# Luna attention and a squared-ReLU layer: batches 0 and 1 loaded together, both attentions first, their hidden tiles in turns

## The chip, the cores and the metric

The kernel runs on one core of a Trainium2 chip. The metric is the device time of one execution in microseconds (us): seven timed runs of the kernel before have a median of 272.58 us (271.35 to 272.79). One further execution was recorded by the hardware profiler; every time of a single instruction in this document comes from such a recorded execution.

The engines of a core work in parallel, each on its own list of instructions, in order. TensorE (PE) multiplies matrices into PSUM, a small memory. ScalarE (ACT) and VectorE (DVE) read PSUM and write SBUF, the large on-chip memory. GpSimd (POOL) here issues the loads, and SyncE (SP) the stores and the transposing transfers. An engine waits for another through semaphores.

## The reference

```python
def sm_attn(qq, kk, vv):
    s = scale * np.matmul(qq, kk.transpose(0, 1, 3, 2))
    s = s - np.max(s, axis=-1, keepdims=True)
    a = np.exp(s)
    a = a / (np.sum(a, axis=-1, keepdims=True) + 1e-09)
    return np.matmul(a, vv)
p_packed = sm_attn(p, k, v)              # 32 packed rows per head
out = sm_attn(q, p_packed, p_packed)     # 576 rows attend to the 32

x = out.transpose(0, 2, 1, 3).reshape(B * S, H * D)
h = x @ w_in
r = np.maximum(h, 0.0)
g = s * (r * r) + b
y = g @ w_out
```

There are 8 batches, 8 heads, 576 rows and 64 columns per head; p has 32 rows per head. x is 4608 x 512, w_in 512 x 2048, w_out 2048 x 512. Inputs and the output are float32, and the loads turn them into bfloat16.

## The kernel before, in words

One batch goes through these helpers; each name stands in the code below.

- `load` (line 93) brings k, q and v of a batch into the SBUF tiles kn, qn and vn, one transfer of 576 KB (as bfloat16) each, on POOL's queue. `load_w_in(ch)` brings a quarter of w_in in two transfers of 256 KB, and `load_w_out(m, m + 4)` a quarter of w_out in one of 512 KB.
- `prep_k` and `prep_q` transpose kn and qn on TensorE, for batches 0 to 2; ACT and DVE copy the result to kT and qT. From batch 3 on, transfers on SP do it (`dma_k`, `dma_q`), from kn and from qr, which is a reordered copy of qn made on DVE (`order_q`; `order_v` does the same for v).
- `first_scores(b, qd)` makes the scores of p against k for half of the heads, and ACT takes the exponential (tile e1). `packed` multiplies by v and DVE writes ppc, with the reciprocal sums rd and rs. `second_scores` makes the scores of q against ppc, and ACT takes the exponential (tile e2). `weights(b, qd)` sums e2 on TensorE, ACT takes Ln (tile ld) and Exp (tile rcd), and DVE multiplies into aT.
- `packed_w1(b, ch)` multiplies ppc by one quarter of w_in, 8 matmuls; the two halves of the result are scaled into pw by ACT and then DVE (both on DVE with `on_act=False`). `packed_w` does two quarters at once.
- `mlp_in(b, m)`, also called through `m1`, makes one of the 16 hidden tiles of a batch: 4 matmuls of 288 columns from pw and aT, ReLU on ACT (tile rlu), the square on DVE (tile gT). The hidden tile m uses quarter m // 4 of pw.
- An `Out` makes 128 rows of y: 16 matmuls of 512 columns over gT and w_out, in steps of any number; then DVE scales and adds (tile ysb) and SP stores. `outs(b)` gives 4 of them for an even batch and 5 for an odd one, and `fill(n)` issues the next n matmuls of those that are waiting.
- `bias_part` sums the rows of w_out, 16 matmuls in all; `idle(n)` issues n matmuls on zeros.

The order on every engine is written by hand: instructions run in program order. Results in PSUM live in `big()` tiles of a pool with three buffers (psh), those of an `Out` in a pool with two (psy). A `big()` tile must be read by ACT or DVE before the third next one can be written.

Lines 128 to 175 give the order of the loads: batch 0, all of w_in, all of w_out, batch 1, then the rest of p. kn, qn, vn, vr and qr have one buffer each, so that a load of the next batch waits for the last reader of the tile before. Eight semaphores are shared by POOL's transfers in turn, so that a transfer also waits for the one eight places ahead of it to land.

Lines 517 to 624 are the beginning, written out step by step: the attention of batch 0, its 16 hidden tiles with the first two Outs and the bias sums between them, then the attention of batch 1 with the remaining two Outs between its steps, its hidden tiles, and the attention of batch 2 between those. From line 626 a loop runs over batches 2 to 7: 16 hidden tiles each, after each hidden tile the steps of the next batch's attention that are set for it, and then `fill(per)`, with per the number of waiting Outs.

Of the kernel before, what the change touches and what calls it, by code (L numbers as in the profile page):

```python
# [14 lines left out]
def kernel(  # L15
# [41 lines left out]

    constp = ctx.enter_context(tc.tile_pool(name="constp", bufs=1))
    wpool = ctx.enter_context(tc.tile_pool(name="wpool", bufs=1))
    rawp = ctx.enter_context(tc.tile_pool(name="rawp", bufs=1))  # L60
    attp = ctx.enter_context(tc.tile_pool(name="attp", bufs=1))
    atp = ctx.enter_context(tc.tile_pool(name="atp", bufs=2))
    smp = ctx.enter_context(tc.tile_pool(name="smp", bufs=2))
# [22 lines left out]
    def big(dt=F32):  # L86
        w = NB if dt == F32 else 2 * NB
        return psh.tile([P, 2, w], dt, tag="h", name="hps")


    kn, qn, vn = {}, {}, {}

    def load(store, src, b, tag, h0=0, h1=H):
        if h0 == 0:
            store[b] = rawp.tile([R, H, NC * D], BF16, tag=tag, name=tag)
        pool.dma_start(
            out=store[b][:, h0:h1, :],
            in_=src[b, h0:h1].rearrange("h (r c) d -> r h (c d)", c=NC),
        )
# [17 lines left out]
    def load_w_out(m0, m1):  # L117
        pool.dma_start(
            out=w_out_sb[:, m0:m1, :],
            in_=moe_w_out[m0 * P:m1 * P, :].rearrange("(m p) d -> p m d", p=P),  # L120
        )
# [17 lines left out]
    bvec = constp.tile([P, 1], F32, name="bvec")  # L139
    sp.dma_start(out=bvec[:], in_=moe_b[0:1].unsqueeze(0).to_broadcast([P, 1]))  # L140
    nc.scalar.preload_act_table_set("natural_log_exp_and_others")
    for ch in range(NCH):
        load_w_in(ch)
    for m in range(0, NFF, 4):
        load_w_out(m, m + 4)

    KW = H * HS + 32
    kT = [constp.tile([P, KW], BF16, name=f"kT{i}") for i in range(2)]
# [17 lines left out]
    def idle(n):  # L166

        t = big()
        for x in range(n):
            mm(t[:, 0, :], zeros[:, 0:P], zeros[:], start=True, stop=True)  # L170

    load(kn, k, 1, "kn")
    load(qn, q, 1, "qn")
    load(vn, v, 1, "vn")
    load_p(2, B)


# [43 lines left out]
        )  # L221

    def order_v(b):
        vr[b] = attp.tile([R, NC, HP, 2, D], BF16, tag="vr", name="vr")
        by_chunk(vr[b], vn[b])

    def order_q(b):
        qr[b] = attp.tile([R, NC, HP, 2, D], BF16, tag="qr", name="qr")
        by_chunk(qr[b], qn[b])

    def prep_q(b, half):
# [53 lines left out]
    def packed(b, qd):  # L285
        i = b % 2
        if qd == 0:
            pps[b] = big()
        pp = pps[b]
        for hp in range(2 * qd, 2 * qd + 2):  # L290
            for c in range(NC):
                if b < N_PE_T:
                    for h2 in range(2):
                        o = hp * 2 * NP + h2 * NP
                        mm(
                            pp[D * h2:D * h2 + D, 0, o:o + NP],
                            vn[b][:, hp + HP * h2, c * D:(c + 1) * D],
                            e1[b][:, h2, c, hp, :],
                            start=(c == 0),
                            stop=(c == NC - 1),  # L300
                            tile_position=(0, D * h2),
                        )
                else:
                    mm(
                        pp[:, 0, hp * 2 * NP:(hp + 1) * 2 * NP],
                        vr[b][:, c, hp, :, :],
                        e1[b][:, :, c, hp, :],
                        start=(c == 0),
                        stop=(c == NC - 1),
                    )  # L310
        for c in range(NC):
            mm(
                pp[:, 1, qd:qd + 1],
                e1[b][:, qd, c, :, :],
                ones1[0:R, :],
                start=(c == 0),
                stop=(c == NC - 1),
            )
        if qd == NQ - 1:
            for h2 in range(2):  # L320
                vec.tensor_copy(
                    out=ppc[i][D * h2:D * h2 + D, :, :],
                    in_=pp[D * h2:D * h2 + D, 0, 0:HP * 2 * NP].rearrange("p (a j) -> p a j", a=HP)[
                        :, :, NP * h2:NP * h2 + NP
                    ],
                )
            rd[b] = smp.tile([P, NQ], F32, tag="rd", name="rd")
            vec.reciprocal(out=rd[b][:], in_=pp[:, 1, 0:NQ])
            rs[b] = smp.tile([P, NQ], F32, tag="rs", name="rs")
            vec.tensor_scalar_mul(out=rs[b][:], in0=rd[b][:], scalar1=scale)  # L330
# [63 lines left out]
    def packed_w1(b, ch, on_act=True):  # L394

        i = b % 2
        if ch == 0:
            pw[b] = ppw.tile([P, NQ, DFF], BF16, tag="pw", name="pw")
        t = big()
        packed_mm(i, ch, [t[:, qd, :] for qd in range(NQ)])  # L400
        dst = pw[b][:, :, ch * NB:(ch + 1) * NB]
        if on_act:
            act.activation(out=dst[:, 0], in_=t[:, 0, :], func=AF.Copy, scale=rd[b][:, 0:1])
        else:
            vec.tensor_scalar_mul(out=dst[:, 0], in0=t[:, 0, :], scalar1=rd[b][:, 0:1])
        vec.tensor_scalar_mul(out=dst[:, 1], in0=t[:, 1, :], scalar1=rd[b][:, 1:2])
# [33 lines left out]
    def bias_part(cps, m):  # L440
        mm(cps, onesb[:], w_out_sb[:, m, :], start=(m == 0), stop=(m == NFF - 1))
        if m == NFF - 1:
            vec.tensor_scalar_mul(out=biasrep[:], in0=cps, scalar1=bvec[:])
# [69 lines left out]
    def m1(b, *ms):  # L513
        for m in ms:
            mlp_in(b, m)
# [16 lines left out]
    packed(0, 1)  # L532
    idle(5)
    second_scores(0)
    packed_w1(0, 0, on_act=False)
    idle(3)
    weights(0, 0)
    weights(0, 1)
    packed_w1(0, 1, on_act=False)
    idle(6)  # L540
    m1(0, 0, 1, 2, 3)
    packed_w1(0, 2, on_act=False)
    m1(0, 4, 5, 6)

    todo = outs(0)
    first, second = todo[0], todo[1]
    bps = big()
    m = 7
    for m0 in range(0, NFF, 4):
        for x in range(m0, m0 + 4):  # L550
            bias_part(bps[:, 0, :], x)
        if m < NFF:
            m1(0, m)
        first.step(4)
        if m < NFF:
            m1(0, m + 1)
        second.step(4)
        if m < NFF:
            m1(0, m + 2)
        if m0 == 0:  # L560
            packed_w1(0, 3, on_act=False)
        m += 3
    loads(2)
    todo = todo[2:]

    def fill(n):
        run_outs(todo, n)

    prep_k(1, 0)
    prep_k(1, 1)  # L570
    fill(4)
    first_scores(1, 0)
    fill(4)
    first_scores(1, 1)
    fill(4)
    prep_q(1, 0)
    prep_q(1, 1)
    fill(4)
    packed(1, 0)
    packed(1, 1)  # L580
    twice_p(2, B)
    fill(5)
    packed_w1(1, 0)
    second_scores(1)
    fill(3)
    packed_w1(1, 1)
    weights(1, 0)
    fill(2)
    weights(1, 1)
    prep_p(2)  # L590
    fill(2)
    packed_w1(1, 2)
    prep_k(2, 0)
    m1(1, 0, 1)
    packed_w1(1, 3)
    m1(1, 2)
    prep_k(2, 1)
    m1(1, 3, 4)
    first_scores(2, 0)
    m1(1, 5, 6)  # L600
    fill(4)
    first_scores(2, 1)
    m1(1, 7, 8)
    prep_q(2, 0)
    prep_q(2, 1)
    m1(1, 9, 10)
    packed(2, 0)
    m1(1, 11)
    packed(2, 1)
    loads(3)  # L610
    m1(1, 12, 13, 14)
    second_scores(2)
    m1(1, 15)
    todo = outs(1)
    packed_w1(2, 0)
    fill(6)
    weights(2, 0)
    fill(4)
    packed_w1(2, 1)
    weights(2, 1)  # L620
    fill(6)
    packed_w1(2, 2)
    fill(4)
    dma_k(3)

    for b in range(2, B):
        a = b + 1
        c = a + 1
        steps = {}

        def at(m, *fs):
            steps.setdefault(m, []).extend(fs)

        d = 3 if b == 2 else 0
        if b == 2:
            at(1, lambda: (packed_w1(2, 3), order_q(3), dma_q(3)))
            at(2, lambda: (prep_p(3), order_v(3)))
        if a < B:
            at(0 + d, lambda: first_scores(a, 0))
            at(1 + d, lambda: first_scores(a, 1))  # L640
            at(3 + d, lambda: packed(a, 0))
            at(4 + d, lambda: packed(a, 1))
            at(6 + d, lambda: second_scores(a))
            at(8 + d, lambda: packed_w(a, 0))
            at(9 + d, lambda: weights(a, 0))
            at(10 + d, lambda: weights(a, 1))
            at(12 + d, lambda: packed_w(a, 1))
        if c < B:
            at(1 + d, lambda: loads(c))
            at(8 + d, lambda: dma_k(c))  # L650
            at(10 + d, lambda: (order_q(c), dma_q(c)))
            at(12 + d, lambda: order_v(c))
            at(14, lambda: prep_p(c))
        if b > 2:
            todo = outs(b - 1)
        per = len(todo)
        for m in range(NFF):
            mlp_in(b, m)
            for f in steps.get(m, []):
                f()  # L660
            fill(per)
        fill(NFF * (NT + 1))
# [31 lines left out]
```

The softmax here doesn't subtract the row's maximum and nothing guards it: scores larger than these inputs give would overflow.

## Time and profile before

| what | us |
|---|---|
| median of 7 runs | 272.58 (271.35 to 272.79) |
| the profiled execution's own time | 270.08 |
| its span, from the first to the last instruction | 268.3 |
| TensorE busy with matmuls in the span | 247.2 (92%) |
| DVE busy | 146.3 (55%) |
| ACT busy | 142.8 (53%) |
| POOL busy | 29.3 (11%) |
| matmuls of the Outs (yps), 544 recorded | 137.2 |
| matmuls of the hidden tiles, 512 recorded | 82.7 |
| matmuls on zeros, 41 recorded | 14.1 |

The span is the time from the first to the last recorded instruction; the execution's own time is 1.8 us longer. Matmuls overlap each other and their ends are modelled, so a group's busy time adds up to more than the time it takes. Where a row of a timeline ends with square brackets, they give how long the engine had been idle before it and what ended the wait. A chain of waits follows the work that ended last back through whatever released each step.

### The profile page before, as it was taken

What the parts mean: (1) busy time and instruction counts of PE and PEld (TensorE: products, weight loads), DVE (VectorE), ACT (ScalarE), POOL (GpSimd) and SP (SyncE); (2) the same over time, 40 slices, a digit from 0 to 9 for tenths busy, and PEclk for the clock granted to TensorE, in tenths of its full rate; (3) what the DMA queues carried; (4) which work ended last, traced back from release to release, by engine and by line L of the source; (5) the groups of instructions that cost most, each with busy time, mean ns of one, the idle gap of its engine ahead of it and who ended that gap; (6) DMA issues with size and microseconds to landing.
All of it is one profiled execution on the core that took longest, in us unless ns stands there. A gap on an engine that the chain in (4) does not pass through costs nothing.

```text
span 268.3 us, 5619 instructions
## 1 busy us (share of the span) xinstructions
PE 247.2 (92%) x2312; PEld 139.5 (52%) x2348; DVE 146.3 (55%) x304; ACT 142.8 (53%) x217; POOL 29.3 (11%) x44
## 2 busy tenths in 40 slices
PE   7787899986989699899999999999999999999993
PEld 2453555644654365465556555665566555555441
DVE  2235854458657745764793559455954574444221
ACT  1045743456977447775855476548753774443000
POOL 8345100211110020030030002000000000000000
PEclk9799999999999999999999999999999999999999
DMA  3999999894792999999979769993731113111332
GB/s 40 197 206 205 205 204 143 148 157 84 129 150 37 184 170 199 128 159 233 168 99 183 194 127 151 125 232 75 132 96 42 39 39 83 39 39 42 78 78 78
DMA packets 54634, 34.32 MB, mean 128 GB/s; under 512 B 27472, under 2 KB 50000, under 8 KB 54608
## 3 DMA queue, kind: packets, MB, share of 16 engines
q0 software_dynamic: 25200, 18.61, 48.1%
q1 hardware_dynamic: 29408, 15.34, 27.4%
q8 instruction: 18, 0.29, 0.4%
q14 instruction: 8, 0.07, 0.1%
HBM read 37.23 MB, written 9.44 MB: 174 GB/s over the span
## 4 chain that ended last, share of the span: by engine, by line
PE 78%; ACT 8%; DVE 5%; DMA 5%; issue 3%; POOL 0%; DVEq 0%; ACTq 0%; POOLq 0%
PE yps L71 42%; PE hps L71 34%; ACT rlu L82 3%; DMA pn<-in_p_dram 3%; PE hps L74 2%; DMA kT<-kn 2%; ACT rcd L82 2%; ACT ld L82 1%; DVE pw L82 1%; ACT e L82 1%; DVE ysb L82 1%; ACT pw L82 1%; DVE qr L82 1%; DVE gT L82 1%; DVE aT L82 1%
## 5 line engine op out<-in xcount | busy, mean ns | idle before, releaser
L71 PE MATMUL yps<-w_out_sb,gT 128*128 128x512 bf16 x544 | 137.2, 379 | 2.8 <-issue 1.6
L82 ACT ACTIVATE rlu<-hps 128x576 bf16<-128x576 f32 x128 | 82.4, 649 | 73.0 <-PE hps L71 65.6
L82 DVE TENSOR_TENSOR gT<-rlu 128x576 bf16<-128x576 bf16 x128 | 58.0, 456 | 70.3 <-ACT rlu L82 69.3
L71 PE MATMUL hps<-aT,pw 128*128 128x288 bf16 x512 | 82.7, 286 | 4.4 <-DVE pbd L82 1.7
L71 PEld LDWEIGHTS <-gT 128*128 128x128 bf16 x576 | 52.8, 98 | 50.2 <-issue 5.8
L71 PEld LDWEIGHTS <-pw 128*128 128x128 bf16 x512 | 49.2, 98 | 39.0 <-issue 4.9
L82 DVE SCALAR_TENSOR_TENSOR ysb<-yps,svec,biasrep 128x512 f32<-128x512 f32 x36 | 26.8, 747 | 14.3 <-PE yps L71 14.0
L82 DVE TENSOR_SCALAR pw<-hps,rd 128x512 bf16<-128x512 f32 (+1 forms) x26 | 24.4, 950 | 3.1 <-ACT pw L82 2.0
L82 ACT ACTIVATE e<-hps 96x768 bf16<-96x768 f32 x16 | 12.8, 802 | 19.4 <-PE hps L71 19.3
L82 ACT ACTIVATE pw<-hps,rd 128x1024 bf16<-128x1024 f32 (+1 forms) x18 | 16.6, 923 | 4.0 <-PE hps L71 3.9
L82 POOL DMA_DIRECT2D kn<-in_k_dram x9 | 6.9, 769 | 104.5 <-DMA kT<-kn 55.2
L82 DVE TENSOR_TENSOR aT<-e,rcd 128x576 bf16<-128x576 bf16 x16 | 12.1, 758 | 10.6 <-ACT rcd L82 10.5
L71 PE MATMUL hps<-zeros 128*128 128x512 bf16 x41 | 14.1, 480 | 2.2 <-DVE zeros L82 1.3
L82 ACT ACTIVATE e<-hps,rs 128x576 bf16<-128x576 f32 x16 | 10.9, 738 | 3.7 <-PE hps L71 3.7
L71 PE MATMUL hps<-w_in_sb,ppc 64*32 64x512 bf16 x256 | 11.6, 383 | 0.9 <-ACT e L82 0.4
L71 PE MATMUL hps<-pbd,kT 128*128 128x64 bf16 x192 | 8.6, 194 | 2.9 <-DMA kT<-kn 2.0
L82 ACT ACTIVATE rcd<-ld 128x576 f32<-128x576 f32 x16 | 10.9, 682 | 0.5
L82 ACT ACTIVATE ld<-hps 128x576 f32<-128x576 f32 x16 | 10.3, 643 | 0.9 <-PE hps L71 0.9
L71 PEld LDWEIGHTS <-kT 128*128 128x128 bf16 x192 | 7.9, 99 | 5.2 <-DMA kT<-kn 2.3
L71 PEld LDWEIGHTS <-ppc 64*32 64x32 bf16 x384 | 4.1, 89 | 9.0 <-issue 7.4
L71 PEld LDWEIGHTS <-zeros 128*128 128x128 bf16 x44 | 4.6, 113 | 7.9 <-issue 4.7
L82 POOL DMA_DIRECT2D qn<-in_q_dram x8 | 6.2, 776 | 12.7 <-PE hps L74 9.6
(45 smaller groups left out, 115.5 us busy)
## 6 DMA issues: line engine op xcount, KB each, us to landing
qn<-in_q_dram POOLq DMA_DIRECT2D x8, 576.0 KB, 10.8
vn<-in_v_dram POOLq DMA_DIRECT2D x8, 576.0 KB, 12.5
out_dram<-ysb SPq DMA_DIRECT2D x24, 192.0 KB, 2.3
kn<-in_k_dram POOLq DMA_DIRECT2D x7, 576.0 KB, 7.3
out_dram<-ysb SPq DMA_DIRECT2D x24, 128.0 KB, 2.5
w_in_sb<-in_moe_w_in_dram POOLq DMA_DIRECT2D x8, 256.0 KB, 12.9
w_out_sb<-in_moe_w_out_dram POOLq DMA_DIRECT2D x4, 512.0 KB, 13.1
out_dram<-ysb SPq DMA_DIRECT2D x24, 64.0 KB, 2.0
```

What stands on the lines that cost most here:

```text
L71: return tc.keep_in_program_order(nc.tensor.matmul(*a, **kw))
L74: return tc.keep_in_program_order(nc.tensor.transpose(*a, **kw))
L82: return lambda *a, **kw: tc.keep_in_program_order(f(*a, **kw))
```

## The change

Three things change in the beginning; the loop over batches 2 to 7 is as it was, but for one call.

First the loads. Batch 1 comes directly after batch 0: kn and qn, then the first quarter of w_in, vn, the first quarter of w_out, and then quarters of w_in and w_out in turns. kn, qn, vn, vr and qr no longer have a buffer each; they draw from one pool of five buffers of the same size.

Then the order of the beginning. After the second scores of batch 0 the attention of batch 1 starts, and the two attentions are interleaved. Of the hidden tiles of batch 0 only four are made before the weights of batch 1; the other twelve alternate with those of batch 1, with two matmuls of an Out (`step(2)`) after ten of the hidden tiles of batch 0. The bias sums come after all the hidden tiles, and the attention of batch 2 after that, between the rest of the first two Outs, the other two Outs of batch 0 and ten matmuls of the Outs of batch 1. `packed_w1` in this part uses ACT for its first half. There are 42 matmuls on zeros where there were 44.

Last, for batches 0 to 2 `packed` writes both halves of the heads to the same columns of PSUM, and one copy of 128 partitions writes ppc instead of two of 64.

```diff
-    rawp = ctx.enter_context(tc.tile_pool(name="rawp", bufs=1))
+    rawp = ctx.enter_context(tc.tile_pool(name="rawp", bufs=5))
...
+    def raw(name):
+        return rawp.tile([R, S // R * DM], BF16, tag="raw", name=name)[:]
+
     def load(store, src, b, tag, h0=0, h1=H):
         if h0 == 0:
-            store[b] = rawp.tile([R, H, NC * D], BF16, tag=tag, name=tag)
+            store[b] = raw(tag).rearrange("r (h x) -> r h x", h=H)
...
-    for ch in range(NCH):
+    load(kn, k, 1, "kn")
+    load(qn, q, 1, "qn")
+    load_w_in(0)
+    load(vn, v, 1, "vn")
+    load_w_out(0, 4)
+    for ch in range(1, NCH):
         load_w_in(ch)
-    for m in range(0, NFF, 4):
-        load_w_out(m, m + 4)
+        load_w_out(4 * ch, 4 * ch + 4)
...
-    load(kn, k, 1, "kn")
-    load(qn, q, 1, "qn")
-    load(vn, v, 1, "vn")
     load_p(2, B)
...
-        vr[b] = attp.tile([R, NC, HP, 2, D], BF16, tag="vr", name="vr")
+        vr[b] = raw("vr").rearrange("r (c h x d) -> r c h x d", c=NC, h=HP, x=2)
...
-        qr[b] = attp.tile([R, NC, HP, 2, D], BF16, tag="qr", name="qr")
+        qr[b] = raw("qr").rearrange("r (c h x d) -> r c h x d", c=NC, h=HP, x=2)
...
-                        o = hp * 2 * NP + h2 * NP
                         mm(
-                            pp[D * h2:D * h2 + D, 0, o:o + NP],
+                            pp[D * h2:D * h2 + D, 0, hp * NP:(hp + 1) * NP],
...
+            if b < N_PE_T:
+                vec.tensor_copy(out=ppc[i][:].rearrange("p a j -> p (a j)"), in_=pp[:, 0, 0:HP * NP])
+            else:
...
     second_scores(0)
-    packed_w1(0, 0, on_act=False)
+    prep_k(1, 0)
+    prep_k(1, 1)
+    weights(0, 0)
+    first_scores(1, 0)
+    weights(0, 1)
+    first_scores(1, 1)
+    loads(2)
     idle(3)
-    weights(0, 0)
-    weights(0, 1)
-    packed_w1(0, 1, on_act=False)
-    idle(6)
-    m1(0, 0, 1, 2, 3)
-    packed_w1(0, 2, on_act=False)
-    m1(0, 4, 5, 6)
-
+    packed_w1(0, 0)
+    prep_q(1, 0)
+    prep_q(1, 1)
+    m1(0, 0, 1)
+    idle(2)
+    packed(1, 0)
+    packed(1, 1)
+    m1(0, 2, 3)
+    second_scores(1)
+    packed_w1(1, 0)
+    idle(2)
     todo = outs(0)
-    first, second = todo[0], todo[1]
-    bps = big()
-    m = 7
-    for m0 in range(0, NFF, 4):
-        for x in range(m0, m0 + 4):
-            bias_part(bps[:, 0, :], x)
-        if m < NFF:
-            m1(0, m)
-        first.step(4)
-        if m < NFF:
-            m1(0, m + 1)
-        second.step(4)
-        if m < NFF:
-            m1(0, m + 2)
-        if m0 == 0:
-            packed_w1(0, 3, on_act=False)
-        m += 3
-    loads(2)
+    t0, t1 = todo[0], todo[1]
     todo = todo[2:]
 
     def fill(n):
         run_outs(todo, n)
 
-    prep_k(1, 0)
-    prep_k(1, 1)
+    weights(1, 0)
+    t0.step(4)
+    weights(1, 1)
+    t1.step(4)
+    packed_w1(0, 1)
+    m1(1, 0)
+    packed_w1(1, 1)
+    m1(1, 1, 2, 3)
+    for c in range(1, NCH):
+        for j in range(4):
+            m1(0, 4 * c + j)
+            if c > 1 or j > 1:
+                (t0 if j % 2 else t1).step(2)
+            m1(1, 4 * c + j)
+            if c + 1 < NCH and j > 1:
+                packed_w1(j - 2, c + 1)
+    twice_p(2, B)
+    bps = big()
+    for m in range(NFF // 2):
+        bias_part(bps[:, 0, :], m)
+    prep_p(2)
+    prep_k(2, 0)
+    for m in range(NFF // 2, NFF):
+        bias_part(bps[:, 0, :], m)
+    prep_k(2, 1)
+    t0.step(4)
+    first_scores(2, 0)
+    t1.step(4)
+    first_scores(2, 1)
     fill(4)
-    first_scores(1, 0)
+    loads(3)
+    prep_q(2, 0)
+    fill(2)
+    prep_q(2, 1)
     fill(4)
-    first_scores(1, 1)
+    packed(2, 0)
     fill(4)
-    prep_q(1, 0)
-    prep_q(1, 1)
-    fill(4)
-    packed(1, 0)
-    packed(1, 1)
-    twice_p(2, B)
-    fill(5)
-    packed_w1(1, 0)
-    second_scores(1)
-    fill(3)
-    packed_w1(1, 1)
-    weights(1, 0)
-    fill(2)
-    weights(1, 1)
-    prep_p(2)
-    fill(2)
-    packed_w1(1, 2)
-    prep_k(2, 0)
-    m1(1, 0, 1)
-    packed_w1(1, 3)
-    m1(1, 2)
-    prep_k(2, 1)
-    m1(1, 3, 4)
-    first_scores(2, 0)
-    m1(1, 5, 6)
-    fill(4)
-    first_scores(2, 1)
-    m1(1, 7, 8)
-    prep_q(2, 0)
-    prep_q(2, 1)
-    m1(1, 9, 10)
-    packed(2, 0)
-    m1(1, 11)
     packed(2, 1)
-    loads(3)
-    m1(1, 12, 13, 14)
+    fill(6)
     second_scores(2)
-    m1(1, 15)
-    todo = outs(1)
-    packed_w1(2, 0)
+    packed_w(2, 0)
     fill(6)
     weights(2, 0)
     fill(4)
-    packed_w1(2, 1)
     weights(2, 1)
-    fill(6)
-    packed_w1(2, 2)
     fill(4)
+    packed_w(2, 1)
     dma_k(3)
+    todo += outs(1)
+    fill(10)
...
         if b == 2:
-            at(1, lambda: (packed_w1(2, 3), order_q(3), dma_q(3)))
+            at(1, lambda: (order_q(3), dma_q(3)))
```

More of the change, by code (lines that the diff above doesn't have):

```diff
@@ L319, in packed @@
         if qd == NQ - 1:
[L320 to L326, printed above, removed]
+            if b < N_PE_T:
+                vec.tensor_copy(out=ppc[i][:].rearrange("p a j -> p (a j)"), in_=pp[:, 0, 0:HP * NP])
+            else:
+                for h2 in range(2):
+                    vec.tensor_copy(
+                        out=ppc[i][D * h2:D * h2 + D, :, :],
+                        in_=pp[D * h2:D * h2 + D, 0, 0:HP * 2 * NP].rearrange("p (a j) -> p a j", a=HP)[
+                            :, :, NP * h2:NP * h2 + NP
+                        ],
+                    )
             rd[b] = smp.tile([P, NQ], F32, tag="rd", name="rd")
```

## The prediction

> **What bounds the kernel now.** First the page: busy shares, and the chain that ended last.
>
> ```profile
> PE 247.2 (92%) x2312; PEld 139.5 (52%) x2348; DVE 146.3 (55%) x304; ACT 142.8 (53%) x217; POOL 29.3 (11%) x44
> PE 78%; ACT 8%; DVE 5%; DMA 5%; issue 3%; POOL 0%; DVEq 0%; ACTq 0%; POOLq 0%
> ```
>
> TensorE has the most work, and the chain runs through it for 78%. Whoever shortens the kernel must remove matmuls or holes between them. The change removes two matmuls on zeros, so I look for holes, by stages.
>
> ```profile
> 20.00:25.00 5.00, 4.15 (x53) 1.90 (x51) 2.39 (x7) 2.79 (x5) 2.84 (x4) 1.00 1.24 203
> 60.00:65.00 5.00, 3.33 (x42) 1.90 (x41) 3.87 (x7) 3.38 (x7) 0.00 (x0) 1.00 0.67 126
> 90.00:95.00 5.00, 2.96 (x38) 1.87 (x37) 3.14 (x9) 2.17 (x4) 1.54 (x3) 1.00 1.02 186
> ```
>
> After the window come the busy times of PE, PEld, DVE, ACT and POOL, then the granted clock, the DMA share and GB/s. Holes lie at 20 to 30, 55 to 80 and 90 to 95 us. From 115 us on TensorE is close to full, and the diff does not touch that part.
>
> Busy time hides part of a hole, since the last matmul's modelled end runs into it. I therefore count from start to start in PE's timeline:
>
> ```profile
> 21.16 0.44 PE L71 MATMUL hps<-qT,ppc 64*32 64x288 bf16 x16
> 42.35 0.65 PE L71 MATMUL hps<-aT,pw 128*128 128x288 bf16 x4
> 42.84 1.03 PE L71 MATMUL yps<-w_out_sb,gT 128*128 128x512 bf16 x4
> 43.71 0.65 PE L71 MATMUL hps<-aT,pw 128*128 128x288 bf16 x4
> ...
> 85.12 0.65 PE L71 MATMUL hps<-aT,pw 128*128 128x288 bf16 x4
> ...
> 92.37 0.52 PE L71 MATMUL hps<-pbd,kT 128*128 128x64 bf16 x12 [1.99 <-DMA kT<-kn]
> ```
>
> A hidden tile costs PE 0.49 us (42.35 to 42.84), four matmuls of an Out 0.87, one 0.216. From the same timeline: packed_w1 0.34, prep_k of a batch 1.02, prep_q 1.16, first scores of a batch 0.7, packed of a batch 1.4, second scores 0.26, packed_w 0.6, one weights 0.25, a matmul on zeros 0.215. At 21.16 batch 0's second scores start; up to there both kernels issue the same. At 85.12 the loop over batches 2 to 7 begins. Between lie 63.96 us, and the items issued sum to 54.3: 32 hidden tiles 15.7, 84 Out matmuls 18.2, 16 bias 3.5, 11 packed_w1 3.8, 9 on zeros 1.9, the attentions 11.2. So 9.6 us are holes, and 2.1 more come at 90.3, where batch 3's kT is late.
>
> **The loads.** POOL's rows show landings, since each transfer waits for the one eight places ahead:
>
> ```profile
> 16.95 0.61 POOL L82 DMA_DIRECT2D w_in_sb<-in_moe_w_in_dram  x1 [2.63 <-DMA vn<-in_v_dram]
> 17.89 0.75 POOL L82 DMA_DIRECT2D w_out_sb<-in_moe_w_out_dram  x1 [0.34 <-DMA w_in_sb<-in_moe_w_in_dram]
> 19.04 0.75 POOL L82 DMA_DIRECT2D w_out_sb<-in_moe_w_out_dram  x1 [0.39 <-DMA w_in_sb<-in_moe_w_in_dram]
> 20.28 0.74 POOL L82 DMA_DIRECT2D w_out_sb<-in_moe_w_out_dram  x1 [0.49 <-DMA w_in_sb<-in_moe_w_in_dram]
> ```
>
> Batch 0's vn lands at 16.95, then one 256 KB piece each 1.25 us, in order: 205 GB/s, which the windows show up to 45 us. 576 KB then take 2.9 us. The new order lands at: kn(1) 19.8, qn(1) 22.7, w_in's first quarter 25.3, vn(1) 28.1, w_out's first 30.7, then a quarter of w_in or w_out each 2.6 us, the last at 46; kn(2) 50, qn(2) and vn(2) by 56, kn(3) and qn(3) by 62. vn(1) takes kn(0)'s buffer, whose last transposes end at 13.2, and POOL issues it then, with over 2 MB still queued: no gap. The pool of five costs nothing, since kn(2) and qn(2) need buffers that are free by 21; vn(3) must wait for kn(2)'s transposes, near 65, and is needed near 85. Needs below: kn(1) 21.4, w_in 26.2, vn(1) 30.4, w_out 35; the least slack is 0.9 us. Bounds of a late load: 0 if these hold; the 2.63 us of POOL's wait for vn(0) is the largest landing wait, so +2.6 at most. I take 0, since the kernel's own landings give the spacing.
>
> **Stage A, 21.16 to the alternating tiles.** PE's items sum to 14.4 us: 8 hidden tiles, 2 steps of 4, 4 packed_w1, both attentions, 5 on zeros. But ACT now has, in strict order, one attention's exponentials beside the other's Ln and Exp:
>
> ```profile
> 23.55 0.65 ACT L82 ACTIVATE ld<-hps 128x576 f32<-128x576 f32 x1 [0.51 <-PE hps L71]
> 24.23 0.68 ACT L82 ACTIVATE rcd<-ld 128x576 f32<-128x576 f32 x1
> 28.84 1.19 ACT L82 ACTIVATE rlu<-hps 128x576 bf16<-128x576 f32 x2 [0.20 <-PE hps L71]
> 57.05 1.36 ACT L82 ACTIVATE e<-hps,rs 128x576 bf16<-128x576 f32 x2
> 58.31 0.69 ACT L82 ACTIVATE pw<-hps,rd 128x512 bf16<-128x512 f32 x1
> ```
>
> From start to start these cost 0.6 to 0.67. ACT's list: 4 e2 2.6, 4 ld and rcd 5.1, 2 e1 (0.81) 1.5, 4 pw 2.4, 2 qT 1.2, 8 rlu 4.7: 17.5 us from 21.67, so it cannot end before 39.2. I walk through it with three PSUM buffers: e2 to 23.0; ld, rcd, e1, ld, rcd, e1 from 23.45 to 27.5; pw and qT to 29.2; two rlu to 30.5; packed(1) 30.4 to 31.9; two rlu to 33.6; e2(1) to 35.0; pw, ld, rcd, ld, rcd to 38.0; pw, rlu, pw and three rlu to 42.2. PE stands still 0.6 to 1.3 us at four places and enters the alternating tiles at 41.55: 6.0 us of holes. The single ppc copy saves one DVE cast of 0.29 per batch, covered by matmuls on zeros at batch 0 and by fills at batch 2, at most 0.3 at batch 1: counted as nothing.
>
> **Stage B, the alternating tiles.** PE: 24 hidden tiles 11.8, 20 Out matmuls 4.3, 4 packed_w1 1.4: 17.5. ACT: 28 × 0.59 to 0.6 = 16.7, just under. Added: 0.4 for the change to packed_w1's shape (0.1 each, 35.07 to 35.66 before), 0.8 for ACT's backlog at entry, and twice 0.6, since batch 1's second-half pw is written by DVE after ACT (0.69 + 0.75) and its first reader comes 0.9 us behind packed_w1. Ends at 61.4; a lower bound with these hidden is 59.1.
>
> **Stage C, to the loop.** Bias 3.5, 46 Out matmuls 10.0 (4 in steps, 32 filled, 10 of batch 1), batch 2's attention and transposes 6.4: 19.9. Batch 2's chain now has the fills between its steps. Waits left: 0.4 at first scores, which read kT's second half (DVE copy 0.75, queued after biasrep), 0.2 for ysb, 0.5 where packed_w needs a buffer of second_scores. Loop entry 61.4 + 21.0 = 82.4 against 85.12, so 2.7 earlier.
>
> **The balance.** At entry 70 Out matmuls of batch 1 are left against 60, and packed_w1(2,3) is done: +2.16 - 0.34 = 1.8 given back. The kT stall: before, DVE's ysb ends 85.80, the stores and dma_k follow, kT is there at 92.37, 6.5 later.
>
> ```profile
> 85.06 0.74 DVE L82 SCALAR_TENSOR_TENSOR ysb<-yps,svec,biasrep 128x512 f32<-128x512 f32 x1
> 85.84 1.11 SPq L82 DMA_DIRECT2D out_dram<-ysb  x2
> 87.06 3.12 SPq L82 DMA_TRANSPOSE kT<-kn  x1
> ```
>
> Now the last ysb of batch 0 ends about 0.2 before the entry (DVE makes it behind aT(2,1)); 6.5 later is 6.3 after entry, while PE arrives after four hidden tiles and three fills of 5, 5.2. About 1.1 of stall stays, 1.0 is saved. At the loop's end the 70 fill only 14 of 16 tiles (60 filled 15), so the wait on DVE's pbd copy there (0.37 before 113.96) is covered less: bounds 0 and the 1.08 of a fill, and I take 0.3, near the row's 0.37. Sum: 2.7 - 1.8 + 1.0 - 0.3 = 1.6 faster; without Stage B's added waits (2.3) 3.9. The profiled execution of 270.08 would be 268.5. It is 2.5 below the median of the timed runs, more than the change itself; carried over to the median, 272.58 - 1.6 = 271.0.
>
> **A rule that speaks against it.** The clock fell to 0.50 at 10 to 13 us, after 6 to 9 us with PE 0.82 of 3 busy; it stayed 1.00 over 90 to 92 us, with 0.39 of 2 busy. Stage A has PE about 70% issued, its longest hole 1.3 us, so I count no loss. [...]
>
> **The rivals.**
> 1. The waits hide better: Stage B near its sum, kT in time. For: 42 to 45 us ran hidden tiles with steps at 1.35 without a hole. Against: ACT's 0.20 gaps at 28.84. Gain 3.0 (part of Stage B's 2.3 back) to 5.0 (all of it, and 1.1 of kT): middle 4.0, 268.6.
> 2. No change: ACT's queue in Stage A costs 1.5 more. Against: ACT's durations vary by under 0.05. 272.6.
> 3. Slower: Stage B bound by the coupling of ACT and PSUM. At 27.45 to 30.26, four ReLUs with a packed_w1 among them took 2.81, 0.70 each. At 0.70 for 24 tiles, with packed_w1 (0.45) and steps not overlapped, 16.8 + 1.8 + 4.3 = 22.9 against 19.9: 3.0 lost, so 1.4 slower, 274.0. It decides once Stage B exceeds 21.5. Against: in 42 to 45 steps did overlap ReLUs.
> 4. The loads don't land as listed (w_in's first quarter or vn(1) over 2.5 late), or the clock falls in Stage A: 0.5 to 1.5 slower, 273.5. For: slack of 0.9 only. Against: in-order landings, full rate.
>
> **How the numbers follow.** Within 0.2% is ±0.55 us, about what a measurement of this kernel can tell from no change. Forecast (gain 0.55 to 3) 0.43; rival 1 0.20; no change 0.11; rival 3 0.16; rival 4 0.10. Faster 0.63, same 0.11, slower 0.26. The range leaves out a tenth at each end: below, the upper half of rival 1, from a gain of 4.3, 268.3; above, rival 3 at its price, 274.0. The forecast's own range is 269.6 to 272.0.
>
> **What would show it.** kn(1) landing near 20 and vn(1) near 28; no hole on DMA over 1 us; loop entry (first hidden tile of batch 2) at 81 to 83; a kT wait near 1 us after it; the clock 1.00 after 14 us. Wrong if PE enters the alternating tiles after 43, if Stage B takes over 21.5, or if anything after batch 2 shifts its pace.

## The result and the profile after

The changed kernel takes 269.12 us (median of 25 runs, 268.6 to 271.3); the kernel before, run beside it, takes 271.0 (median of 60, 269.66 to 273.18). The ratio is 0.9925, with a 95% interval of 0.9906 to 0.9944: 1.5 to 2.5 us faster. The profiled execution after takes 268.97 with a span of 267.2, against 270.08 and 268.3: 1.1 us. The two gains differ because the timed runs of before fall into two groups, 34 of the 60 near 270.6 and 26 near 272.6, and the profiled execution belongs to the shorter; the last section says what parts them. Here and below, a ratio to the kernel before leaves out runs that are over 1.5% above the fastest run of the same kernel.

Busy shares and the chain that ended last, from the page of the kernel after:

```profile
PE 246.7 (92%) x2307; PEld 139.7 (52%) x2346; DVE 143.0 (54%) x295; ACT 144.4 (54%) x219; POOL 29.6 (11%) x44
PE 70%; DMA 9%; ACT 8%; DVE 7%; issue 4%; POOL 0%; DVEq 0%; ACTq 0%; POOLq 0%
```

Apart from the two matmuls on zeros TensorE's work is the same; for the rest only holes can have moved. Windows of the kernel after, in us from the span's start, with the columns as before (width; busy PE, PEld, DVE, ACT, POOL; granted clock; DMA share; GB/s):

```profile
20.00:25.00 5.00, 4.09 (x71) 2.62 (x71) 2.20 (x6) 3.24 (x5) 1.74 (x4) 1.00 1.28 203
60.00:65.00 5.00, 5.00 (x38) 2.74 (x36) 2.98 (x8) 1.57 (x3) 0.00 (x0) 1.00 0.05 8
90.00:95.00 5.00, 4.95 (x56) 3.20 (x55) 1.73 (x4) 2.65 (x5) 0.70 (x1) 1.00 1.12 156
110.00:120.00 10.00, 8.03 (x95) 5.11 (x97) 7.54 (x16) 5.80 (x9) 1.53 (x2) 1.00 0.82 127
```

At 60 to 65 us PE is full (3.33 busy before), and so it is at 90 to 95 (2.96 before). A new hole stands at 110 to 120, where before had 8.96 busy. PE's timeline of the kernel after names the holes:

```profile
20.73 0.44 PE L71 MATMUL hps<-qT,ppc 64*32 64x288 bf16 x16
...
49.24 0.91 PE L71 MATMUL hps<-aT,pw 128*128 128x288 bf16 x6 [0.37 <-DVE pw L82]
...
56.45 0.91 PE L71 MATMUL hps<-aT,pw 128*128 128x288 bf16 x6 [0.37 <-DVE pw L82]
...
60.94 1.89 PE L71 MATMUL hps<-w_out_sb,onesb 128*128 128x512 bf16 x8
...
82.64 0.65 PE L71 MATMUL hps<-aT,pw 128*128 128x288 bf16 x4
...
88.65 0.51 PE L71 MATMUL hps<-pbd,kT 128*128 128x64 bf16 x12 [0.54 <-DVE pbd L82]
...
109.35 0.65 PE L71 MATMUL hps<-aT,pw 128*128 128x288 bf16 x4
...
112.84 0.65 PE L71 MATMUL hps<-aT,pw 128*128 128x288 bf16 x4 [1.48 <-DVE pbd L82]
113.33 0.51 PE L71 MATMUL hps<-pbd,kT 128*128 128x64 bf16 x12
...
151.05 0.44 PE L71 MATMUL hps<-qT,ppc 64*32 64x288 bf16 x16 [0.33 <-DMA qT<-qr]
```

The same places in PE's timeline of the kernel before:

```profile
111.58 0.65 PE L71 MATMUL hps<-aT,pw 128*128 128x288 bf16 x4
...
113.96 0.65 PE L71 MATMUL hps<-aT,pw 128*128 128x288 bf16 x4 [0.37 <-DVE pbd L82]
114.81 0.51 PE L71 MATMUL hps<-pbd,kT 128*128 128x64 bf16 x12 [0.20 <-ACT pw L82]
...
152.12 0.44 PE L71 MATMUL hps<-qT,ppc 64*32 64x288 bf16 x16
```

Batch 0's second scores start at 20.73, the alternating tiles end where the bias sums begin, at 60.94, and the loop begins at 82.64. Behind the second scores that is 61.91 us, against 63.96 before: 2.05 earlier. The wait of the first scores inside the loop is 0.54 against 1.99. The wait at the loop's end is 1.48 against 0.37. Batch 3's first hidden tile starts at 112.84 against 113.96, and batch 4's first scores, 92.60 behind the second scores, come 1.05 earlier than before (114.81 - 21.16 = 93.65). From there on both kernels issue the same, but they do not wait the same. With the 0.43 us by which the startup of this execution is shorter, batch 4's first scores come 1.48 earlier in all; batch 5's second scores come only 1.07 earlier (151.05 against 152.12), and the span is 1.1 shorter. The 0.4 goes at these scores. The transposing transfer of their qT was issued at 134.05 and landed 16.9 us later, and PE waited 0.33 for it; before, it was issued at 135.52 and landed after 15.3 us, with 1.3 to spare. A second recording of the kernel after waits 0.83 at the same place.

### The profile page after: what moved, and what is told of

Its sections match the earlier page's. It is cut to its first block, busy times and chain, and to the rows that moved or that the text cites. A ratio compares the mean times of both kernels' runs of the same rounds, so it can differ in the third digit from the quotient of the medians.

```text
span 267.2 us, 5606 instructions
## 1 busy us (share of the span) xinstructions
PE 246.7 (92%) x2307; PEld 139.7 (52%) x2346; DVE 143.0 (54%) x295; ACT 144.4 (54%) x219; POOL 29.6 (11%) x44
## 4 chain that ended last, share of the span: by engine, by line
PE 70%; DMA 9%; ACT 8%; DVE 7%; issue 4%; POOL 0%; DVEq 0%; ACTq 0%; POOLq 0%
PE yps L71 38%; PE hps L71 30%; DMA qT<-qr 6%; DMA pn<-in_p_dram 2%; PE hps L74 2%; ACT rlu L82 2%; DVE pw L82 2%; ACT rcd L82 2%; ACT pw L82 2%; DVE qr L82 2%; ACT ld L82 1%; ACT e L82 1%; DVE gT L82 1%; DVE ysb L82 1%; DVE kT L82 1%
## 5 line engine op out<-in xcount | busy, mean ns | idle before, releaser
L82 DVE TENSOR_SCALAR pw<-hps,rd 128x1024 bf16<-128x1024 f32 (+1 forms) x20 | 21.3, 1067 | 4.6 <-ACT pw L82 2.0
L82 ACT ACTIVATE pw<-hps,rd 128x1024 bf16<-128x1024 f32 (+1 forms) x20 | 18.8, 940 | 0.8 <-PE hps L71 0.7
L71 PE MATMUL hps<-zeros 128*128 128x512 bf16 x36 | 13.1, 486 | 2.5 <-DVE zeros L82 1.3
L82 POOL DMA_DIRECT2D vn<-in_v_dram x8 | 6.2, 777 | 41.7 <-PE hps L74 27.7
```

Source lines behind the costliest of these rows:

```text
L71: return tc.keep_in_program_order(nc.tensor.matmul(*a, **kw))
L82: return lambda *a, **kw: tc.keep_in_program_order(f(*a, **kw))
```

## The experiments

The theory: the beginning gained some 2 us because batch 1's waits are covered, the stall for batch 3's keys shrank, and part went again because more Out matmuls wait at the loop and run out sooner. Rivals: the loads alone or the order alone do it; another producer than kT holds the first scores; ACT does not bound the new beginning; the gain is the clock's.

**The kernel before once more.**

> The kernel before, unchanged, to see the granted clock beside each time. Its runs so far lie in two groups, near 270.5 and near 272.6, the changed kernel's nearly all near 269.1. If the granted clock makes the groups: the runs near 272.6 show a mean clock lower by about 0.01 to 0.02 than those near 270.5 (2 us more at half clock is 0.008 to 0.015 of the span). If something else does (landings of loads): the clock is the same in both groups, within 0.004.

Measured: 271.84 (median of 12, 269.31 to 272.7). Its profiled execution is one of the long ones: 272.7, with a mean clock of 0.981 where the profile shown before had 0.994. Windows of this execution, the same columns:

```profile
90.72:94.13 3.41, 1.32 (x19) 0.76 (x17) 3.25 (x8) 0.88 (x2) 0.00 (x0) 1.00 0.96 176
94.13:97.55 3.42, 3.20 (x21) 1.97 (x21) 0.46 (x1) 1.95 (x3) 2.30 (x3) 0.50 1.04 131
```

The wait of 2.09 us for kT ends at 93.34, and at 94.13 the clock falls to half for 3.4 us. It falls in the same way at 63.41, behind the wait of 1.34 for DVE's pbd copy near 62. The profile shown before had both waits and no fall there. So behind the two holes that the change closes (the second) or shortens (the first) more was lost in this execution than their own length, about 1.3 us with each fall (worked out in the last section).

**The loads alone, the order alone.** The first is the kernel before with only the new loads and the shared buffers, the second the kernel after with the old order of loads.

```diff
 (before, loads alone)
+    load(kn, k, 1, "kn")
+    load(qn, q, 1, "qn")
+    load_w_in(0)
+    load(vn, v, 1, "vn")
+    load_w_out(0, 4)
-    for ch in range(NCH):
+    for ch in range(1, NCH):
         load_w_in(ch)
...
 (after, order alone)
-    for ch in range(1, NCH):
+    for ch in range(NCH):
         load_w_in(ch)
-        load_w_out(4 * ch, 4 * ch + 4)
+    for m in range(0, NFF, 4):
+        load_w_out(m, m + 4)
...
+    load(kn, k, 1, "kn")
+    load(qn, q, 1, "qn")
+    load(vn, v, 1, "vn")
     load_p(2, B)
```

> Only the new load order and the shared pool of five buffers, with the old order of the work. Theory (the loads only make the new order possible): slower. The first packed_w1 of batch 0 stands until w_in's first quarter lands near 25, and the second until near 33, where it ran at 23.7 before, so the first hidden tile starts near 35 instead of 27: 7 to 9 us slower, near 279. Rival (the loads are what gains): 269 to 270.

> Only the new order of the work (and the single ppc copy), with the old load order: batch 1 behind all weights. Theory: TensorE stands at the transposes of batch 1's k from 21 until it lands near 39.5: about 18 us slower than the changed kernel, near 287. Rival (the order of the work gains whatever the loads do): within 3 us of 269.

Measured: 281.14 and 288.24, one run each. PE's timeline with the loads alone:

```profile
23.43 0.39 PE L71 MATMUL hps<-w_in_sb,ppc 64*32 64x512 bf16 x1 [1.30 <-DMA w_in_sb<-in_moe_w_in_dram]
24.69 0.62 PE L71 MATMUL hps<-w_in_sb,ppc 64*32 64x512 bf16 x7 [0.88 <-DMA w_in_sb<-in_moe_w_in_dram]
...
31.43 0.61 PE L71 MATMUL hps<-w_in_sb,ppc 64*32 64x512 bf16 x1 [3.76 <-DMA w_in_sb<-in_moe_w_in_dram]
```

and with the order alone:

```profile
39.68 1.54 PE L74 MATMUL hps<-identb,kn 96*128 96x96 bf16 x17 [17.70 <-DMA kn<-in_k_dram]
```

With the loads alone the old order asks for w_in's first two quarters by 31 us, while they now come behind 1.2 and 1.7 MB of batch 1; the new order with the old loads asks for kn(1) at 21 and gets it at 39.7. Each half alone loses 10 to 17 us, at a lower clock than before (mean 0.963 and 0.964). The loads are worth nothing by themselves; they allow the order. The single copy of ppc, the third part of the change, was not run by itself; in order alone it came along with the new order.

**What holds the first scores at 88.65.** The profile names pbd; the prediction had named kT alone. One kernel starts the transfer of kT earlier, the other makes pbd earlier.

```diff
 (kT early)
     weights(2, 0)
+    dma_k(3)
     fill(4)
...
     packed_w(2, 1)
-    dma_k(3)
     todo += outs(1)
...
 (pbd early)
     dma_k(3)
+    prep_p(3)
...
-            at(2, lambda: (prep_p(3), order_v(3)))
+            at(2, lambda: order_v(3))
...
-            at(14, lambda: prep_p(c))
+            at(5, lambda: prep_p(c))
```

> The changed kernel with batch 3's transposing transfer of k issued two fills earlier, ahead of the last store of batch 0. In the changed kernel TensorE stands 0.7 us before batch 3's first scores, near 88. If the late kT holds it: the hole goes, 0.5 to 0.7 faster than the changed kernel, 268.4 to 268.6. If DVE's copy of pbd, which ends at 88.50, holds it: no change, 269.1.

> The changed kernel with prep_p(3) moved ahead of the loop and every later prep_p from the 15th hidden tile of a batch to the 6th, so that DVE's pbd copies no longer queue behind the reordered copies of q and v. The earlier transfer of kT left the hole before batch 3's first scores (0.7 us near 88) as it was. If the pbd copy holds that hole and the one of 1.48 at batch 3's first hidden tile: both shrink, the first to under 0.2 and the second by 0.5 to 1.5; 267.0 to 268.4. If something else on DVE or ACT is late there in its place: 268.8 to 269.4, with holes of the same size under another name.

Measured: kT early 271.3 (median of 12, 267.41 to 277.63), ratio 0.9945 (0.9904 to 0.9986); pbd early 268.55 (median of 4), ratio 0.9891 (0.9825 to 0.9958). PE's timeline with kT early:

```profile
89.81 0.51 PE L71 MATMUL hps<-pbd,kT 128*128 128x64 bf16 x12 [0.54 <-DVE pbd L82]
```

The transfer was issued at 76.99 instead of 83.48, and the hole did not move: batch 3's first hidden tile stands 92.11 us behind the second scores in both kernels. Its median of 271.3 is above that of the kernel after: five of the twelve runs have a mean clock of 0.966 to 0.981, and in its profiled execution the clock was half for 6.8 us in the startup and for another 3.4 us from 114.0 on. The run of 273.34, at a mean clock of 0.991, is not explained by that. With pbd early:

```profile
89.66 0.52 PE L71 MATMUL hps<-pbd,kT 128*128 128x64 bf16 x12 [0.42 <-DMA kT<-kn]
...
113.12 0.51 PE L71 MATMUL hps<-pbd,kT 128*128 128x64 bf16 x12 [0.62 <-ACT pw L82]
```

Now kT holds the first scores, a little shorter; and the 1.48 at the loop's end is gone, 0.62 for pw is left. Batch 4's first scores come 1.34 earlier than in the kernel after. So both producers end at nearly the same moment: the first scores start 67.92 us behind the second scores when pbd holds them and 67.80 when kT does. The loop's end was held by pbd, which DVE makes late behind its other work. By the medians alone pbd early cannot be told from the kernel after, nor can the next two kernels; what each of them moved is read from its profile.

**Do the Out matmuls run out too soon?**

```diff
-        per = len(todo)
+        per = 4 if b == 2 else len(todo)
```

> The changed kernel with four Out matmuls behind each hidden tile of batch 2 instead of five, so that all 16 tiles have some and 6 are left for the end. If the bare last two tiles lay open the wait at batch 3's first hidden tile (1.48 us near 112 in the changed kernel, 0.37 before): that hole falls under 0.6 and the time by 0.7 to 1.1, to 268.0 to 268.4. If that wait only moves to other places of the loop: 269.1. If holes of over 1.5 us there also let the clock fall in some executions, the spread to 271 goes as well.

Measured: 269.21 (median of 10), ratio 0.99 (0.9868 to 0.9933): the time of the kernel after. PE's timeline:

```profile
89.16 0.52 PE L71 MATMUL hps<-pbd,kT 128*128 128x64 bf16 x12 [1.36 <-DMA kT<-kn]
...
109.76 0.62 PE L71 MATMUL hps<-w_in_sb,ppc 64*32 64x512 bf16 x15 [0.42 <-ACT rlu L82]
...
123.93 0.44 PE L71 MATMUL hps<-qT,ppc 64*32 64x288 bf16 x16 [0.97 <-DMA qT<-qr]
```

The 1.48 at the loop's end is gone, so the missing fills had uncovered it. But with 4 fills instead of 5 in each step PE reaches the first scores sooner and waits 1.36 for kT, and later 0.97 for qT. Batch 4's first scores come 0.7 earlier, its second scores 0.3 later than in the kernel after. Holes moved from one late producer to the next.

**The two waits for pw among the alternating tiles.**

```diff
-            if c + 1 < NCH and j > 1:
-                packed_w1(j - 2, c + 1)
+            if c + 1 < NCH and j in (1, 2):
+                packed_w1(j - 1, c + 1)
```

> The changed kernel with each packed_w1 of the alternating tiles one pair of tiles earlier. Theory: the two holes of 0.37 (near 49 and 56), where the first tile of batch 1 in a quarter waits for DVE's half of pw, go; the alternating tiles get 0.6 to 0.8 shorter, 268.4. Rival (ACT and PSUM bound that stretch): the same 0.7 turns up as waits of the tiles on ACT, 269.1.

Measured: 268.46 (median of 8), ratio 0.9873 (0.9837 to 0.9909). Both waits of 0.37 are gone, and so is one of 0.40 for a ReLU at 44.63. Batch 2's first scores stand 43.96 behind the second scores instead of 45.24: 1.28 earlier, twice the 0.6 to 0.8 expected. PE's timeline shows the stretch that had waited at 49.24, now without a bracket:

```profile
48.83 0.59 PE L71 MATMUL yps<-w_out_sb,gT 128*128 128x512 bf16 x2
49.26 1.14 PE L71 MATMUL hps<-aT,pw 128*128 128x288 bf16 x8
50.24 0.59 PE L71 MATMUL yps<-w_out_sb,gT 128*128 128x512 bf16 x2
```

**Is the new beginning bound by ACT?** This kernel leaves out seven matmuls on zeros, 1.5 us of PE, and compares with a second recording of the kernel after; the second scores start at 21.26 and 21.25.

```diff
     loads(2)
-    idle(3)
     packed_w1(0, 0)
...
     m1(0, 0, 1)
-    idle(2)
     packed(1, 0)
...
     packed_w1(1, 0)
-    idle(2)
     todo = outs(0)
```

> The changed kernel without the seven matmuls on zeros behind the second scores of batch 0; they take TensorE 1.5 us. If ACT's queue sets the interleaved attentions: the alternating tiles begin at the same distance behind batch 0's second scores (20.5 us, within 0.3), the time stays within 0.4 of the changed kernel. If TensorE's own work sets them: 1.0 to 1.5 faster. If the zeros hold the clock up: it falls to 0.5 between 25 and 45 us, and the kernel is 1 to 2 slower.

> The changed kernel unchanged, on the same chip as the others of this call: 269.0 to 269.6, with some executions near 271.3 at a mean clock of about 0.978, where the clock has fallen once more than in the others.

Measured: 268.58 (two runs, 268.49 and 268.66) against 269.03 (median of 10, 267.43 to 271.55, ratio to before 0.9895, 0.9863 to 0.9928). The entry into the alternating tiles, PE's timeline of the kernel after recorded again:

```profile
41.39 0.77 PE L71 MATMUL hps<-aT,pw 128*128 128x288 bf16 x5 [0.43 <-ACT rlu L82]
```

and without the seven matmuls:

```profile
40.93 1.26 PE L71 MATMUL hps<-aT,pw 128*128 128x288 bf16 x9 [0.43 <-ACT rlu L82]
```

0.46 of the 1.5 us comes back, a little more than expected. Most of the rest turns into waits for ACT's exponentials (0.71 instead of 0.16 between the two halves of prep_q) and for DVE's aT (a new 0.54), which needs ACT's rcd. ACT bounds this stage, though not wholly. A fall of the clock without these matmuls does not show: the mean was 0.991 in both runs, as in the profile of the kernel after, and the 24 matmuls of 288 columns from 40.93 take 3.12 us, as they do there from 40.89.

**The kernel before with kT alone moved.** Before, the transfer of batch 3's keys stands behind the last `fill(4)` ahead of the loop.

```diff
     packed_w1(2, 0)
+    dma_k(3)
     fill(6)
...
     fill(4)
-    dma_k(3)
```

> The kernel before with one line moved: batch 3's transposing transfer of k is issued behind packed_w1(2, 0) instead of behind the fills. Theory: of the 2.1 us that TensorE stood for kT near 90 some 1.3 go, until DVE's pbd copy ends near 91.0: 1.3 faster in the profile, and the granted clock no longer falls near 94, so that the median falls from about 271.4 to 269.2 to 269.8: most of what the whole change gains. Rival (the hole was covered by slack behind it): within 0.5 of the kernel before.

> The kernel before with the one line moved (batch 3's transfer of kT earlier), timed anew. In its profile batch 4's first scores come 92.5 us behind batch 0's second scores, against 93.65 before and 92.60 in the changed kernel. If that distance is what counts: the same time as the changed kernel of this call within 0.8, about 269.5, and few executions near 272.6, since the hole after which the clock fell near 94 is gone. If the changed order has worth beyond it: 270.5 or more.

Measured: the first time 269.81, 276.22, 276.92 and 279.12; the second time, of 12 runs, seven took 268.45 to 271.67 (ratio 0.9916, 0.9877 to 0.9954, from these) and five 275.46 to 277.8. PE's timeline of the run of 269.81:

```profile
92.06 0.51 PE L71 MATMUL hps<-pbd,kT 128*128 128x64 bf16 x12 [0.73 <-ACT rlu L82]
```

kT no longer holds the scores, and batch 4's first scores come 92.48 behind the second scores, 1.17 earlier than before. One moved transfer has as much as the whole change (1.05). But 8 of the 16 runs are 6 to 10 us longer. The profile of one of them (276.12), PE's timeline:

```profile
105.73 0.68 PE L71 MATMUL hps<-qT,ppc 64*32 64x288 bf16 x16 [3.76 <-DMA qT<-qr]
```

Its transposing transfer for qT was issued at 91.13 beside the loads of qn(4) at 91.28 and vn(4) at 93.19 and landed 14.6 us later; then the clock was 0.55 to 0.60 over 104 to 112. In the execution of 269.81 the same three were issued at 91.20, 91.36 and 93.27, and PE did not wait. Why the transfer is late in some executions stays open.

**All three improvements together.** The kernel after with pw early, pbd early and kT early.

```diff
+            if c + 1 < NCH and j in (1, 2):
+                packed_w1(j - 1, c + 1)
...
     weights(2, 0)
+    dma_k(3)
...
     packed_w(2, 1)
-    dma_k(3)
+    prep_p(3)
...
+            at(2, lambda: order_v(3))
...
+            at(5, lambda: prep_p(c))
```

> The changed kernel with three moves together: packed_w1 one pair earlier (the first scores of batch 2 came 1.28 us earlier with it), prep_p earlier (batch 4's first scores 1.34 us earlier), and batch 3's transfer of kT two fills earlier. With kT early alone DVE's pbd copy held batch 3's first scores, with pbd early alone kT did, both near the same time, so that the two together should take the 0.6 us which neither took alone. Sum 3.2 faster than the changed kernel: 265.7 to 266.5. If the gains overlap, or come back as a wait further on (qT of batch 3 or 4): 267.0 to 267.8.

Measured: 266.92 (median of 6, 266.06 to 271.07), ratio 0.982 (0.9773 to 0.9867): about 5 us below before, and 2.1 below the kernel after timed beside it. PE's timeline:

```profile
87.14 0.51 PE L71 MATMUL hps<-pbd,kT 128*128 128x64 bf16 x12
...
110.58 0.51 PE L71 MATMUL hps<-pbd,kT 128*128 128x64 bf16 x12 [0.62 <-ACT pw L82]
```

The hole at the first scores is gone only now that both kT and pbd are early. Batch 4's first scores come 89.38 behind the second scores, against 92.59 in the kernel after recorded beside it: 3.21 earlier. The median is 0.4 above the 265.7 to 266.5 that were expected.

## Why the prediction was right, and where not

The direction, the range and nearly the gain came out: 2.0 us between the medians against 1.6. The time of 269.12 is 1.9 below the 271.0 predicted, and below the likeliest case's own range, mostly because the 60 runs of before have a median of 271.0 and not 272.58. In the two profiles the schedule gave 1.05 up to batch 4's first scores and not 1.6, and 0.4 of it was lost again at batch 5's second scores; the clock gave most of the rest. So part of the agreement is luck.

*Loads: right.* POOL's rows of the kernel after:

```profile
19.57 0.75 POOL L82 DMA_DIRECT2D w_out_sb<-in_moe_w_out_dram  x1 [2.31 <-DMA kn<-in_k_dram]
22.74 0.62 POOL L82 DMA_DIRECT2D w_in_sb<-in_moe_w_in_dram  x1 [2.42 <-DMA qn<-in_q_dram]
...
28.05 0.62 POOL L82 DMA_DIRECT2D w_in_sb<-in_moe_w_in_dram  x1 [2.49 <-DMA vn<-in_v_dram]
```

kn(1), qn(1) and vn(1) land at 19.57, 22.74 and 28.05, where 19.8, 22.7 and 28.1 were worked out from the spacing of before. PE waits for no load from DRAM behind 20 us; rival 4 did not come.

*Stage A: right.* The alternating tiles begin about 20.65 us behind the second scores (20.4 predicted). The walk along ACT's list carried this; a sum of PE's items alone gave 14.4. (Its list names 5 matmuls on zeros; the kernel issues 7 there, which ACT's list covers.)

*Stage B: right in the sum, not in each term.* It ends 40.21 behind the second scores (40.24 predicted). The two waits for pw were there at 0.37 each instead of 0.6, and taking them away also freed the 0.40 at 44.63. Rival 3, a pace set by ACT and PSUM together, did not come: in 46 to 60 us the steps ran between hidden tiles without other holes.

*Stage C: 21.7 against 21.0.* packed_w waited 0.66 (0.5 predicted). The remaining 0.5 is spread over the stage and belongs to no row of its own. The loop so begins 2.05 earlier, not 2.7: this term was too large by 0.65.

*Given back, 1.8: right.* It is in the count of fills, ten more.

*The kT stall: the size near, the reason only half.* From the end of the fourth hidden tile to the first scores it took 0.70, against 2.15 before: 1.45 saved where 1.0 was predicted. The prediction took kT for the only late operand. The two kernels above show two of them, kT and pbd, 0.12 us apart: moving kT alone left the hole as it was.

*The loop's end: the term that was mis-sized.* The prediction bounded the uncovered pbd wait by 0 and 1.08 and took 0.3, near the row's 0.37. From the last hidden tile of batch 2 to the first of batch 3 it is 3.49 against 2.38: 1.11 lost, a little over the bound. The row of before was already covered by a fill; its 0.37 was what was left, not the size of the wait. With per = 4 in place of 5, or pbd made earlier, it was gone.

The sum to batch 3's first tile: 2.05 - 1.8 + 1.45 - 1.11 = 0.59, measured 0.69; batch 4's first scores add 0.36, since their wait of 0.20 for pw is gone: 1.05 in place of 1.6. Rival 1, the waits hidden better, came at kT alone and was outweighed at the loop's end; rival 2, a Stage A longer by 1.5, did not come.

*Behind batch 2: a term left at nothing.* The prediction took TensorE as close to full from 115 us on, and untouched because the diff is not there. The wait of 0.33 for qT at batch 5's second scores (0.83 in the second recording) shows that it was touched: PE comes earlier, and the transfer does not land earlier with it (at 150.95, against 150.8 before).

*The clock: missing from the sum.* The prediction asked whether new holes would lower it in Stage A (they did not, 1.00 from 15 us until the last matmuls are done), and not whether the old holes lowered it in executions other than the one profiled. Its carrying over of a difference between two profiles to a median of 272.58 was therefore a step with a gap: seven runs, six of them near 272.6, are a sample of the long group.

## What to carry to other kernels

Size an uncovered wait from when its producer ends, not from the stall that is left in a schedule where something covers it. Where an instruction reads two late operands, the profile names one; a gain needs both moved, and moving them one at a time shows nothing or little. Where the timed runs fall into two groups, compare the clocks of these before carrying a difference of two profiles over to the median, and count a hole on TensorE of the size seen here (1.3 to 2.1 us) at its own length plus what the clock may take (about 1.3 us for a stretch of half clock here).

## What the runs showed of the hardware

The half clock came in whole stretches of about 3.4 us: one in the profile of before (9.70 to 13.11 us, mean 0.994), three in the long execution of before_again (0.981, and 3 x 3.4 / 2 / 270.9 is 0.019). Of 65 timed runs of the kernel before beside the experiments, the 38 above 271.9 have mean clocks of 0.977 or 0.981, and the 27 below it 0.983 to 1.00. The changed kernel has 2 of 25 runs at 0.977, both at 271.3, and the rest at 0.985 to 0.998 near 269.1. Between the two profiles of before (270.08 and 272.7), two more stretches go with 2.6 us more, about 1.3 each. At a like clock the two kernels are about 1 us apart: with a mean of 0.994, four timed runs of before took 269.75 to 270.37, and six of the changed kernel 268.94 to 269.98, five of them at most 269.14. So the 2.0 of the medians is about 1 of schedule, and the rest is mostly that fewer executions of the changed kernel lose the clock; a split to the tenth isn't shown, since the startup also differs by up to 1.4 us between executions (second scores at 20.7 to 22.1).

Behind the new hole at the loop's end the clock fell too, in two of the recorded executions. Windows of the kernel with kT early, columns as above:

```profile
110.60:114.00 3.40, 1.56 (x22) 0.62 (x20) 3.23 (x8) 2.36 (x4) 0.70 (x1) 1.00 0.10 20
114.00:117.40 3.40, 3.18 (x20) 1.94 (x21) 3.02 (x5) 1.45 (x2) 0.84 (x2) 0.50 1.03 171
```

PE was busy for 1.56 of 3.4 us, with a longest hole of 1.48, and the next 3.4 us had half the clock; in the profile of the kernel after, the same hole stayed without a fall. With pw early it fell too, at 113.12, after 3.41 us with 1.57 busy.

In both recorded executions of the kernel before, the stretches start whole multiples of 3.413 us apart. In the long one the three start at 8.80, 63.41 and 94.13: 54.61 and 30.72 apart, 16 and 9 times 3.413. In the profile of before one starts at 9.70 and one behind the last instruction, at 269.11: 259.41 apart, 76 times 3.413. If such steps are counted on from these starts, an estimate of the author's, the hole for kT lay within one step of the long execution (1.32 of 3.41 busy, shown above), and across two steps of the other:

```profile
88.20:91.62 3.42, 2.19 (x16) 1.19 (x13) 3.25 (x9) 1.49 (x3) 0.00 (x0) 1.00 0.97 174
91.62:95.03 3.41, 2.60 (x34) 1.79 (x36) 1.59 (x4) 1.55 (x3) 1.57 (x3) 1.00 1.04 190
```

The prediction's 0.39 of 2 busy at 90 to 92, where the clock stayed, lay across these two. The steps were read from these traces and not set by an experiment, and what decides behind which of them the clock falls was not shown.
